# Shared PSUM banks for two partial sums, a later third block, and a gate in three pieces, in a spectral layer with a feed-forward network

## The chip, the cores and the metric

The kernel runs on one NeuronCore of one Trainium2 chip. The metric is the device time of one execution in microseconds (us), as the median of several runs. The engines are called by the profile's names: PE (matmul), PEld (the loading of PE's weights), DVE (vector), ACT (scalar), POOL (GpSimd) and SP (issues DMAs).

## What is computed

```
X = rfft(x, axis=1)                       # x is (8, 3008, 256)
Yr = Xr @ w_r - Xi @ w_i + b_r ; Yi = Xr @ w_i + Xi @ w_r + b_i
Yr, Yi = soft threshold of both at 0.01
y = irfft(Yr + 1j * Yi, n=3008, axis=1)
h = y.reshape(24064, 256) @ moe_w_in      # to 2048 features
out = (h * clip(h + 3, 0, 6) / 6) @ moe_w_out
```

All numbers are float32. The kernel keeps that precision by splitting every operand of a large product into a rounded part (`hi`) and a rest (`lo`) and by adding three matmuls (weight lo by hi, hi by lo, hi by hi, in this order) (`product`, line 137).

## The kernel before

There are two kinds of work. The *spectral* work makes `y`: for each of the 8 batches `stage1`, `middle` and `segment` do the transforms as matmuls with small tables, through the PSUM pool `ps_a`. The *units* are the feed-forward network: 47 tiles of 512 tokens by 8 pairs of 128-feature blocks, 376 units in all.

A unit's first product (256 inputs to 256 features, for 512 tokens) is a 2x2 by 2x2 product of blocks, done with seven block products in place of eight (`block(i, n, ...)`, n from 1 to 7, as in Winograd's form of Strassen's method). Each is three matmuls of 128x128 by 256 columns. `prepare` makes the seven right sides `yb` once for each tile.

- Blocks 1, 6, 7 and 4 add up in one PSUM tile, `pb`. ACT copies what stands in it after block 1 (`p1`), after 6 (`u2`), after 7 (`u3`, line 563) and after 4 (a quarter of `h`, line 594).
- Block 2 goes to the PSUM tile `pd`; DVE adds `p1` to it (a quarter of `h`, line 566).
- Block 5 goes to the PSUM tile `pc`; DVE adds `u3` (another quarter). Block 3 is then added onto `pc`; DVE adds `u2` (the last quarter).

DVE's three additions are called the p1 add, the u3 add and the u2 add below. When the four quarters of `h` are there, the *gate* follows (`gate`, a generator that is advanced at chosen places): ACT makes `r` = relu(h + 3) (line 601), DVE makes min(r, 6)·h (line 603), ACT rounds it to `gs` hi (line 130), and DVE makes the rest, `gs` lo (line 131, called the gs subtraction). A unit's second product is four *down products* (`down(i, u, dh)`), each of three matmuls of 512 columns into `po0` or `po1`; the first and the third go to `po0`, the others to `po1`. The first matmul of a down product reads `gs` hi, the second reads `gs` lo, the third `gs` hi again.

The loop at the end works on several units in one step: in step i it runs phases a and b of unit i (blocks 2, 1, then 6), phases c and d of unit i-1 (blocks 7, 5, then 4, 3), and the down products of unit i-3. `fill` puts spectral work between them. The text's order is a priority only: the framework's scheduler orders each engine's instructions by what its own model holds ready, the earlier in the text first, and fixes that order in the program. On the chip each engine then takes its queue in that order, and an instruction that waits for a semaphore holds all behind it.

PSUM has eight banks, and all are given out: `pb` two, `pd` one, `pc` one, `po0` and `po1` one each, `ps_a` two. A tile that is freed is given to the next of its name when all that read it have ended.

Of the kernel before, what the change touches and what calls it, by code (L numbers as in the profile page):

```python
# [9 lines left out]
F32 = mybir.dt.float32  # L10
# [5 lines left out]
PSUM = bass.MemoryType.PSUM  # L16
# [9 lines left out]
P = 128  # L26
# [7 lines left out]
H = T // 2  # L34
# [66 lines left out]
def spectral_ffn(ctx: ExitStack, tc: tile.TileContext, x, w_r, w_i, bias, w_in, w_out, f47, f64, g64, sgn, out):  # L101
    nc = tc.nc
# [1 line left out]
    sb = ctx.enter_context(tc.tile_pool(name="sb", bufs=1))  # L104
    dram = ctx.enter_context(tc.tile_pool(name="dram", bufs=2, space=DRAM))
    ps_b = ctx.enter_context(tc.tile_pool(name="ps_b", bufs=2, space=PSUM))
    ps_c = ctx.enter_context(tc.tile_pool(name="ps_c", bufs=1, space=PSUM))
    ps_o = ctx.enter_context(tc.tile_pool(name="ps_o", bufs=1, space=PSUM))
    ps_a = ctx.enter_context(tc.tile_pool(name="ps_a", bufs=2, space=PSUM))

# [3 lines left out]
    def space(shape, dt, name, tag=None):  # L114
        tag = tag or name
        return sb.tile(shape, dt, name=name, tag=tag, bufs=depth.get(tag, 1))
# [11 lines left out]
    def split(hi, lo, src, on=None):  # L128

        nc.scalar.copy(out=hi, in_=src)  # L130
        (on or nc.vector).tensor_tensor(out=lo, in0=src, in1=hi.bitcast(F32), op=ALU.subtract)  # L131

    def product(ps, terms, start=True, stop=True, more=False):

        todo = [p for (ah, al), (bh, bl) in terms for p in ((al, bh), (ah, bl), (ah, bh))]
        for n, (a, b) in enumerate(todo):
            nc.tensor.matmul(  # L137
                out=ps,
                lhsT=a,
                rhs=b,  # L140
                start=start and n == 0,
                stop=stop and n == len(todo) - 1,
                skip_group_check=more,
            )
# [100 lines left out]
    def turn(how=None):  # L245

        for job in list(busy):
            if next(job[0], busy) is busy:
                busy.remove(job)
                ready.add(job[1])  # L250
        if how and made[0] < 2 * nf:
            make, f = next(bands)
            g = make(f, how[made[0] % len(how)])
            next(g)
            busy.append((g, (make, f)))
            made[0] += 1
# [298 lines left out]
    hs, ps_of, keep, gs, pos = {}, {}, {}, {}, {}  # L555

    def block(i, n, ps, start):
        c, f = units[i]
        product(ps, [(tuple(t[:, f, WEIGHT[n]] for t in win_s), yb[c, n])], start=start, more=True)

    def kept(i, n, ps):
        t = keep[i, n] = space([P, H], F32, n)
        nc.scalar.copy(out=t, in_=ps)  # L563

    def added(i, u, half, ps, n):
        nc.vector.tensor_tensor(out=hs[i][:, u, half * H : (half + 1) * H], in0=ps, in1=keep.pop((i, n)), op=ALU.add)  # L566

    def phase_a(i):
        pb = ps_b.tile([P, 512], F32, name="pb")[:, :H]
        pd = ps_c.tile([P, 512], F32, name="pd")[:, :H]  # L570
        ps_of[i] = pb
        hs[i] = space([P, 2, T], F32, "h")
        block(i, 2, pd, True)
        block(i, 1, pb, True)
        kept(i, "p1", pb)
        added(i, 0, 0, pd, "p1")

    def phase_b(i):
        block(i, 6, ps_of[i], False)
        kept(i, "u2", ps_of[i])  # L580

    def phase_c(i):
        pc = ps_c.tile([P, 512], F32, name="pc")[:, :H]
        block(i, 7, ps_of[i], False)
        block(i, 5, pc, True)
        kept(i, "u3", ps_of[i])
        added(i, 1, 1, pc, "u3")
        keep[i, "pc"] = pc

    def phase_d(i):  # L590
        pb, pc = ps_of.pop(i), keep.pop((i, "pc"))
        block(i, 4, pb, False)
        block(i, 3, pc, False)
        nc.scalar.copy(out=hs[i][:, 1, :H], in_=pb)  # L594
        added(i, 0, 1, pc, "u2")

    def gate(i):

        h = hs.pop(i)
        r = space([P, 2, T], F32, "r")  # L600
        nc.scalar.activation(out=r, in_=h, func=AF.Relu, bias=three, scale=1.0)  # L601
        yield
        nc.vector.scalar_tensor_tensor(out=r, in0=r, scalar=6.0, in1=h, op0=ALU.min, op1=ALU.mult)  # L603
        t = gs[i] = space([P, 2, 2, T], F32R, "gs")
        split(t[:, 0], t[:, 1], r)
        yield

    def down(i, u, dh):
        c, f = units[i]
        ft = 2 * f + u  # L610
        first, last = f == 0 and u == 0, f == nf - 1 and u == 1
        if first:
            pos[dh] = ps_o.tile([P, 512], F32, name=f"po{dh}")
        g = gs[i]
        product(
            pos[dh],
            [(part(wout_s, slice(ft * D + dh * P, ft * D + (dh + 1) * P)), (g[:, 0, u], g[:, 1, u]))],
            start=first,
            stop=last,
        )  # L620
        if last:
            ot = space([P, T], F32, "ot")
            if dh:
                nc.vector.tensor_scalar(out=ot, in0=pos[dh], scalar1=1.0 / 6.0, scalar2=None, op0=ALU.mult)
            else:
                nc.scalar.mul(out=ot, in_=pos[dh], mul=1.0 / 6.0)
            nc.sync.dma_start(out=out[dh * P : (dh + 1) * P, c * T : (c + 1) * T], in_=ot)
# [57 lines left out]
    def fill(q):  # L685
        turn(LATE if q % 2 == 0 else None)
        for g in slots.get(q, []):
            next(g, None)

    gates = {}  # L690

    def gated(i):
        if i in gates:
            next(gates[i], None)

    n = len(units)
    for i in range(n + 3):
        for kind, f in ((in_band, i), (out_band, i - 3)):
            while 0 <= f < nf and (kind, f) not in ready:
                turn(LATE)  # L700
        if i < n:
            phase_a(i)
        gated(i - 2)
        fill(4 * i)
        if 0 <= i - 3 < n:
            down(i - 3, 0, 0)
        if 0 <= i - 1 < n:
            phase_c(i - 1)
        fill(4 * i + 1)
        if 0 <= i - 3 < n:  # L710
            down(i - 3, 0, 1)
        if i < n:
            phase_b(i)
        fill(4 * i + 2)
        if 0 <= i - 3 < n:
            down(i - 3, 1, 0)
        if 0 <= i - 1 < n:
            phase_d(i - 1)
            gates[i - 1] = gate(i - 1)
            gated(i - 1)  # L720
        fill(4 * i + 3)
        if 0 <= i - 3 < n:
            down(i - 3, 1, 1)
            gs.pop(i - 3)


def words(w):
# [42 lines left out]
```

## Time and profile before

| what | value |
|---|---|
| median of 3 runs (lowest, highest) | 2685.37 us (2683.7, 2688.47) |
| profiled execution: span from first to last instruction | 2685.1 us |
| mean granted clock of PE | 0.983 |
| busy: PE, PEld, DVE, ACT, POOL | 2575.2, 2304.1, 1975.0, 1845.8, 809.6 us |
| first matmul into `pd` (the first unit) | at 146 us |

The profiled execution has no time beside its span; the span lies 0.3 us below the median of the runs. Until about 470 us the first units run between the spectral work of the first batches and the decoding of the weights. From there to about 2300 us units and spectral work alternate, and behind 2300 us little but units is left. A row of a timeline gives the start, the duration, the engine, the line, the operation with out<-in, the shapes and how many instructions were merged; in brackets stands how long the engine was idle before it and what ended that.

### The profile page before, as it was taken

What the parts mean: (1) busy time and instruction counts of PE and PEld (TensorE: products, weight loads), DVE (VectorE), ACT (ScalarE), POOL (GpSimd) and SP (SyncE); (2) the same over time, 40 slices, a digit from 0 to 9 for tenths busy, and PEclk for the clock granted to TensorE, in tenths of its full rate; (3) what the DMA queues carried; (4) which work ended last, traced back from release to release, by engine and by line L of the source; (5) the groups of instructions that cost most, each with busy time, mean ns of one, the idle gap of its engine ahead of it and who ended that gap; (6) DMA issues with size and microseconds to landing.
All of it is one profiled execution on the core that took longest, in us unless ns stands there. A gap on an engine that the chain in (4) does not pass through costs nothing.

```text
span 2685.1 us, 44479 instructions
## 1 busy us (share of the span) xinstructions
PE 2575.2 (96%) x16432; PEld 2304.1 (86%) x16432; DVE 1975.0 (74%) x3192; ACT 1845.8 (69%) x3631; POOL 809.6 (30%) x772
## 2 busy tenths in 40 slices
PE   5778998999999999999999999999999999999999
PEld 4667887898899888898898888989888999999997
DVE  7766885777777777777777777777777777766666
ACT  5666666676777777677776777676667666677765
POOL 4254333233313432333322433243232122121210
PEclk8879999999999999999999999999999999999999
DMA  6623433232222331223222322132222121101000
GB/s 198 188 61 98 125 105 95 77 83 72 76 72 70 83 88 55 73 80 85 74 61 72 87 81 67 58 90 78 77 66 65 56 60 50 48 24 31 16 20 17
DMA packets 150178, 199.98 MB, mean 74 GB/s; under 512 B 16847, under 2 KB 104135, under 8 KB 149959
## 3 DMA queue, kind: packets, MB, share of 16 engines
q1 hardware_dynamic: 149959, 197.13, 25.6%
q8 instruction: 129, 2.11, 0.3%
q14 instruction: 90, 0.74, 0.1%
HBM read 97.45 MB, written 74.97 MB: 64 GB/s over the span
## 4 chain that ended last, share of the span: by engine, by line
PE 68%; DVE 11%; ACT 8%; issue 4%; POOL 3%; DMA 3%; SPq 0%; ACTq 0%; DVEq 0%; POOLq 0%
PE po L137 28%; PE pb L137 15%; PE ps_a L137 9%; PE pc L137 8%; PE pd L137 4%; ACT r L601 3%; DVE r L603 3%; ACT gs L130 2%; PE ps_a L502 2%; DVE gs L131 2%; PE ps_a L377 2%; DMA xin<-in_x 2%; DVE h L566 2%; DVE X L131 1%; DVE tc L427 1%
## 5 line engine op out<-in xcount | busy, mean ns | idle before, releaser
L137 PE MATMUL po<-gs,w_out_hi 128*128 128x512 f32 x3008 | 950.1, 396 | 1.0 <-DVE gs L131 1.0
L603 DVE SCALAR_TENSOR_TENSOR r<-r,h 128x1024 f32<-128x1024 f32 x376 | 476.0, 1266 | 382.8 <-ACT r L601 382.4
L137 PEld LDWEIGHTS po<-gs,w_out_hi 128*128 128x128 f32 x3008 | 568.3, 189 | 68.8 <-DVE gs L131 2.2
L137 PE MATMUL po<-gs,w_out_lo 128*128 128x512 f32 x1504 | 606.2, 403 | 1.7 <-ACT gs L130 1.7
L137 PE MATMUL pb<-yb,w_in_hi 128*128 128x256 f32 x3008 | 598.9, 280 | 1.8 <-POOL yb L131 1.8
L131 DVE TENSOR_TENSOR gs<-r,gs 128x1024 fp32r<-128x1024 f32 x376 | 477.9, 1271 | 131.6 <-ACT gs L130 128.4
L601 ACT ACTIVATE r<-h,three 128x1024 f32<-128x1024 f32 x376 | 433.2, 1152 | 201.5 <-DVE h L566 198.4
L137 PEld LDWEIGHTS pb<-yb,w_in_hi 128*128 128x128 f32 x3008 | 464.5, 189 | 51.2 <-POOL yb L131 2.1
L130 ACT CAST gs<-r 128x1024 fp32r<-128x1024 f32 x376 | 396.0, 1053 | 137.0 <-DVE r L603 129.2
L131 POOL TENSOR_TENSOR yb<-T,yb 128x256 fp32r<-128x256 f32 x188 | 208.6, 1120 | 764.0 <-ACT yb L130 763.9
L137 PE MATMUL pb<-yb,w_in_lo 128*128 128x256 f32 x1504 | 427.2, 284 | 7.4 <-ACT h L594 5.0
L566 DVE TENSOR_TENSOR h<-pc,u 128x256 f32<-128x256 f32 x752 | 313.8, 417 | 67.0 <-PE pc L137 63.5
L137 PEld LDWEIGHTS pb<-yb,w_in_lo 128*128 128x128 f32 x1504 | 284.3, 189 | 65.8 <-ACT h L594 6.6
L563 ACT COPY u<-pb 128x256 f32<-128x256 f32 x752 | 276.5, 372 | 90.5 <-PE pb L137 86.5
L137 PE MATMUL pc<-yb,w_in_hi 128*128 128x256 f32 x1504 | 298.7, 280 | 1.4 <-POOL yb L131 1.4
L137 PEld LDWEIGHTS po<-gs,w_out_lo 128*128 128x128 f32 x1504 | 284.2, 189 | 10.4 <-ACT gs L130 2.3
L137 PE MATMUL pc<-yb,w_in_lo 128*128 128x256 f32 x752 | 217.8, 290 | 15.2 <-DVE h L566 14.7
L137 PEld LDWEIGHTS pc<-yb,w_in_hi 128*128 128x128 f32 x1504 | 230.1, 190 | 2.1 <-POOL yb L131 1.6
L594 ACT COPY h<-pb 128x256 f32<-128x256 f32 x376 | 140.7, 374 | 122.4 <-PE pb L137 120.4
L137 PEld LDWEIGHTS pc<-yb,w_in_lo 128*128 128x128 f32 x752 | 141.9, 189 | 35.0 <-DVE h L566 32.4
L131 POOL TENSOR_TENSOR xs<-xin,xs 120x512 fp32r<-120x512 f32 (+1 forms) x45 | 59.1, 1313 | 352.4 <-ACT xs L130 290.6
L566 DVE TENSOR_TENSOR h<-pd,p 128x256 f32<-128x256 f32 x376 | 156.8, 417 | 7.3 <-ACT p L563 4.6
(129 smaller groups left out, 4018.0 us busy)
## 6 DMA issues: line engine op xcount, KB each, us to landing
bt<-scr SPq DMA_DIRECT2D x96, 256.0 KB, 3.0
scr<-pt SPq DMA_DIRECT2D x96, 256.0 KB, 2.0
zt<-tc SPq DMA_DIRECT2D x376, 64.0 KB, 2.0
out<-ot SPq DMA_DIRECT2D x94, 256.0 KB, 2.1
xin<-in_x SPq DMA_DIRECT2D x48, 480.0 KB, 4.5
scr<-a SPq DMA_DIRECT2D x96, 240.0 KB, 2.5
qt<-scr SPq DMA_DIRECT2D x96, 240.0 KB, 3.5
f<-in_f SPq DMA_DIRECT2D x96, 128.0 KB, 2.9
```

The source lines that it names most:

```text
L130: nc.scalar.copy(out=hi, in_=src)
L131: (on or nc.vector).tensor_tensor(out=lo, in0=src, in1=hi.bitcast(F32), op=ALU.subtract)
L137: nc.tensor.matmul(out=ps, lhsT=a, rhs=b, start=start and n == 0, stop=stop and n == len(todo) - 1, skip_group_check=more,)
L377: nc.tensor.matmul(out=psv[:, dh, :, u, :], lhsT=data[:, u, dh * P : (dh + 1) * P], rhs=f[:, u, :], start=True, stop=True,)
L427: nc.vector.tensor_tensor(out=t, in0=t, in1=c, op=ALU.subtract)
L502: nc.tensor.matmul(out=ps[:, cs * w + g * rows : cs * w + (g + 1) * rows], lhsT=qt[:rows, cs, g, dh * P : (dh + 1) * P], rhs=f47_s[2][:row ...
L563: nc.scalar.copy(out=t, in_=ps)
L566: nc.vector.tensor_tensor(out=hs[i][:, u, half * H : (half + 1) * H], in0=ps, in1=keep.pop((i, n)), op=ALU.add)
L594: nc.scalar.copy(out=hs[i][:, 1, :H], in_=pb)
L601: nc.scalar.activation(out=r, in_=h, func=AF.Relu, bias=three, scale=1.0)
L603: nc.vector.scalar_tensor_tensor(out=r, in0=r, scalar=6.0, in1=h, op0=ALU.min, op1=ALU.mult)
```

## The change

1. `pd` and `pc` of a unit become the two halves of one tile of one bank, and there are two such banks (pool `ps_c` with `bufs=2`), one for odd and one for even units.
2. Block 3 moves out of phase d into a new phase e, which stands behind the step's last down product; the u2 add and the start of the gate move with it. The copy of `pb` to `h` stays in phase d.
3. The gate has a second `yield`: its middle (DVE's min and product) is asked for behind phase c, and its third piece (the rounding to `gs` hi and the gs subtraction) behind phase b. Before, both were asked for behind phase a.

```
-    ps_c = ctx.enter_context(tc.tile_pool(name="ps_c", bufs=1, space=PSUM))
+    ps_c = ctx.enter_context(tc.tile_pool(name="ps_c", bufs=2, space=PSUM))
...
     def phase_a(i):
         pb = ps_b.tile([P, 512], F32, name="pb")[:, :H]
-        pd = ps_c.tile([P, 512], F32, name="pd")[:, :H]
+        both = ps_c.tile([P, 512], F32, name="pc")
+        pd, keep[i, "pc"] = both[:, :H], both[:, H:]
...
     def phase_d(i):
-        pb, pc = ps_of.pop(i), keep.pop((i, "pc"))
+        pb = ps_of.pop(i)
         block(i, 4, pb, False)
-        block(i, 3, pc, False)
         nc.scalar.copy(out=hs[i][:, 1, :H], in_=pb)
+
+    def phase_e(i):
+        pc = keep.pop((i, "pc"))
+        block(i, 3, pc, False)
         added(i, 0, 1, pc, "u2")
...
         nc.vector.scalar_tensor_tensor(out=r, in0=r, scalar=6.0, in1=h, op0=ALU.min, op1=ALU.mult)
+        yield
         t = gs[i] = space([P, 2, 2, T], F32R, "gs")
...
             phase_a(i)
-        gated(i - 2)
         fill(4 * i)
...
             phase_c(i - 1)
+        gated(i - 2)
...
             phase_b(i)
+        gated(i - 2)
...
             phase_d(i - 1)
-            gates[i - 1] = gate(i - 1)
-            gated(i - 1)
         fill(4 * i + 3)
         if 0 <= i - 3 < n:
             down(i - 3, 1, 1)
             gs.pop(i - 3)
+        if 0 <= i - 1 < n:
+            phase_e(i - 1)
+            gates[i - 1] = gate(i - 1)
+            gated(i - 1)
```

No instruction is added or removed on any engine; the order and the waits change. First, PE's queue from block 3 of a unit k (number 154, near the middle of the program) on, before (the first matmul of block 3 stands just ahead of the first row): block 3 in `pc_14133`, the fourth down product of unit k-2, blocks 2 and 1 of unit k+2, the first down product of unit k-1, block 7 and the start of block 5 of unit k+1.

```order
L137 MATMUL pc_14133<-yb_13743,w_in_hi_78 128x256 x2
L137 MATMUL po1_14150<-gs_14038,w_out_lo_81 128x512
L137 MATMUL po1_14150<-gs_14038,w_out_hi_80 128x512 x2
L137 MATMUL pd_14179<-yb_13512,w_in_lo_79 128x256
L137 MATMUL pd_14179<-yb_13512,w_in_hi_78 128x256 x2
L137 MATMUL pb_14178<-yb_13553,w_in_lo_79 128x256
L137 MATMUL pb_14178<-yb_13553,w_in_hi_78 128x256 x2
L137 MATMUL po0_14129<-gs_14114,w_out_lo_81 128x512
L137 MATMUL po0_14129<-gs_14114,w_out_hi_80 128x512 x2
L137 MATMUL pb_14101<-yb_13619,w_in_lo_79 128x256
L137 MATMUL pb_14101<-yb_13619,w_in_hi_78 128x256 x2
L137 MATMUL pc_14200<-yb_13677,w_in_lo_79 128x256
```

The last row, block 5 of unit k+1, is the first that needs the u2 add of unit k, and the program has a wait for DVE there. The same place now, with the waits shown; block 2 of unit k+2 is `pc_14024`:

```order
L137 MATMUL po1_13992<-gs_13922,w_out_lo_81 128x512
L137 MATMUL po1_13992<-gs_13922,w_out_hi_80 128x512 x2
L137 MATMUL pc_13873<-yb_13593,w_in_lo_79 128x256 [waits DVE_49]
L137 MATMUL pc_13873<-yb_13593,w_in_hi_78 128x256 x2
L137 MATMUL pb_14023<-yb_13402,w_in_lo_79 128x256 [waits Activation_49]
L137 MATMUL pb_14023<-yb_13402,w_in_hi_78 128x256 x2
L137 MATMUL po0_13971<-gs_14001,w_out_lo_81 128x512
L137 MATMUL po0_13971<-gs_14001,w_out_hi_80 128x512 [waits DVE_49]
L137 MATMUL pc_14024<-yb_13365,w_in_lo_79 128x256 [waits DVE_49]
L137 MATMUL pc_14024<-yb_13365,w_in_hi_78 128x256 x2
L137 MATMUL po0_13971<-gs_14001,w_out_hi_80 128x512
```

Block 3 (`pc_13873`) now stands behind the fourth down product, and the first that needs its u2 add is block 2 of unit k+2 (`pc_14024`, the same bank), with block 1 and two down matmuls between them.

Second, DVE's queue at the u2 add of the same unit k, now. It stands so before, too, except that the p1 add and the min-and-product stood the other way round:

```order
L131 TENSOR_TENSOR gs_14001<-r_13945,gs_14001 128x1024 [waits Activation_49]
L131 TENSOR_TENSOR z_14068<-zt_13788,z_14068 128x512 [waits DMAHW1_49,DMAHW2_49,DMAHW0_49,DMAHW3_49,PE_49,Activation_49]
L566 TENSOR_TENSOR h_13874<-pc_13873,u2_13920 128x256 [waits PE_49]
L566 TENSOR_TENSOR h_14025<-pc_14024,p1_14032 128x256 [waits PE_49,Activation_49]
L606 SCALAR_TENSOR_TENSOR r_14021<-r_14021,h_13874 128x1024 [waits Activation_49]
```

The gs subtraction of unit k-1 and a piece of spectral work (`z`) stand ahead of the u2 add (`u2_13920`).

Third, ACT's queue near the program's end, where there is no spectral work, before:

```order
L601 ACTIVATE r_29684<-h_29573,three_75 128x1024 [waits DVE_49,Activation_49]
L563 COPY p1_29698<-pb_29689 128x256 [waits PE_49]
L563 COPY u3_29718<-pb_29630 128x256 [waits PE_49]
L130 CAST gs_29702<-r_29684 128x1024 [waits DVE_49]
L563 COPY u2_29727<-pb_29689 128x256 [waits PE_49]
L594 COPY h_29632<-pb_29630 128x256 [waits PE_49]
```

and now:

```order
L563 COPY p1_29333<-pb_29324 128x256 [waits PE_49]
L563 COPY u3_29348<-pb_29266 128x256 [waits PE_49,Activation_49]
L604 ACTIVATE r_29322<-h_29210,three_75 128x1024 [waits DVE_49,Activation_49]
L563 COPY u2_29358<-pb_29324 128x256 [waits PE_49]
L130 CAST gs_29360<-r_29322 128x1024 [waits DVE_49]
L593 COPY h_29268<-pb_29266 128x256 [waits PE_49]
```

The copies `p1` and `u3` moved ahead of the gate's relu, and the copy `u2` of unit k+2 moved ahead of the gate's rounding (`CAST`) of unit k.

More of the change, by code (lines that the diff above doesn't have):

```diff
@@ L106, in spectral_ffn @@
     ps_b = ctx.enter_context(tc.tile_pool(name="ps_b", bufs=2, space=PSUM))
-    ps_c = ctx.enter_context(tc.tile_pool(name="ps_c", bufs=1, space=PSUM))
+    ps_c = ctx.enter_context(tc.tile_pool(name="ps_c", bufs=2, space=PSUM))
     ps_o = ctx.enter_context(tc.tile_pool(name="ps_o", bufs=1, space=PSUM))
@@ L569, in phase_a @@
         pb = ps_b.tile([P, 512], F32, name="pb")[:, :H]
-        pd = ps_c.tile([P, 512], F32, name="pd")[:, :H]
+        both = ps_c.tile([P, 512], F32, name="pc")
+        pd, keep[i, "pc"] = both[:, :H], both[:, H:]
         ps_of[i] = pb
@@ L582, in phase_c @@
     def phase_c(i):
-        pc = ps_c.tile([P, 512], F32, name="pc")[:, :H]
+        pc = keep[i, "pc"]
         block(i, 7, ps_of[i], False)
@@ L587, in phase_c, with phase_e @@
         added(i, 1, 1, pc, "u3")
-        keep[i, "pc"] = pc
     def phase_d(i):
-        pb, pc = ps_of.pop(i), keep.pop((i, "pc"))
+        pb = ps_of.pop(i)
         block(i, 4, pb, False)
+        nc.scalar.copy(out=hs[i][:, 1, :H], in_=pb)
+    def phase_e(i):
+        pc = keep.pop((i, "pc"))
         block(i, 3, pc, False)
-        nc.scalar.copy(out=hs[i][:, 1, :H], in_=pb)
         added(i, 0, 1, pc, "u2")
@@ L603, in gate @@
         nc.vector.scalar_tensor_tensor(out=r, in0=r, scalar=6.0, in1=h, op0=ALU.min, op1=ALU.mult)
+        yield
         t = gs[i] = space([P, 2, 2, T], F32R, "gs")
@@ L702, in spectral_ffn @@
             phase_a(i)
-        gated(i - 2)
         fill(4 * i)
@@ L708, in spectral_ffn @@
             phase_c(i - 1)
+        gated(i - 2)
         fill(4 * i + 1)
@@ L713, in spectral_ffn @@
             phase_b(i)
+        gated(i - 2)
         fill(4 * i + 2)
@@ L718, in spectral_ffn @@
             phase_d(i - 1)
-            gates[i - 1] = gate(i - 1)
-            gated(i - 1)
         fill(4 * i + 3)
@@ L724, in spectral_ffn @@
             gs.pop(i - 3)
+        if 0 <= i - 1 < n:
+            phase_e(i - 1)
+            gates[i - 1] = gate(i - 1)
+            gated(i - 1)
 def words(w):
```

## The prediction

> **What bounds the kernel now.** I read the shares of the page first, then the busy time by stretch, then the list of waits for PE and for its weight loading in the long middle stretch, and last single steps in the timeline.
>
> ```profile
> PE 2575.2 (96%) x16432; PEld 2304.1 (86%) x16432; DVE 1975.0 (74%) x3192; ACT 1845.8 (69%) x3631; POOL 809.6 (30%) x772
> ...
> 0.00:146.00 146.00, 92.20 (x494) 75.94 (x494) 107.48 (x174) 86.27 (x168) 60.11 (x64) 0.81 0.65 189
> 146.00:470.00 324.00, 291.17 (x1752) 254.53 (x1753) 231.65 (x363) 210.03 (x427) 126.37 (x115) 0.94 0.34 95
> 470.00:2300.00 1830.00, 1812.75 (x11780) 1632.80 (x11779) 1373.63 (x2247) 1284.67 (x2541) 551.23 (x511) 1.00 0.25 72
> 2300.00:2685.00 385.00, 379.10 (x2412) 340.82 (x2410) 262.22 (x411) 264.85 (x497) 71.86 (x82) 1.00 0.07 24
> ```
>
> The columns behind the length of a stretch are busy time of PE, PEld, DVE, ACT and POOL, then clock and DMA. From 470 us on PE is busy all but 23 us of 2215 (17.25 and 5.9). So PE's stream bounds the kernel, and an edit that only moves work can win what PE waits, and can lose whatever new waits it puts into that stream. What PE waits for between 470 and 2300 us, as the matmuls see it and as the weight loads ahead of them see it (total, times, longest):
>
> ```profile
> PE pc L137 <- DVE h L566: 12.5, 32, 1.1
> ...
> PEld pc L137 <- DVE h L566: 28.2, 56, 1.3
> PEld pb L137 <- ACT u L563: 4.4, 11, 0.9
> PEld pb L137 <- ACT p L563: 3.5, 11, 0.6
> PEld pb L137 <- ACT h L594: 2.4, 5, 0.8
> ```
>
> One wait stands out: a `pc` block that waits for an addition on DVE. It is block 3 waiting for the u3 add, as in the step at 1244 us:
>
> ```profile
> 1243.93 0.41 DVE L566 TENSOR_TENSOR h<-pc,u 128x256 f32<-128x256 f32 x1
> 1244.39 0.19 PEld L137 LDWEIGHTS pc<-yb,w_in_lo 128*128 128x128 f32 x1 [0.52 <-DVE h L566]
> 1244.40 0.39 PE L137 MATMUL pc<-yb,w_in_lo 128*128 128x256 f32 x1 [0.33 <-DVE h L566]
> ```
>
> The add ends at 1244.34 and PE goes on 0.06 us later. Now a step near the end, without spectral work:
>
> ```profile
> 2630.62 1.27 DVE L131 TENSOR_TENSOR gs<-r,gs 128x1024 fp32r<-128x1024 f32 x1 [0.45 <-ACT gs L130]
> 2630.64 0.28 PE L137 MATMUL pc<-yb,w_in_lo 128*128 128x256 f32 x1
> ...
> 2631.69 0.28 PE L137 MATMUL pd<-yb,w_in_lo 128*128 128x256 f32 x1
> 2631.80 0.41 DVE L566 TENSOR_TENSOR h<-pc,u 128x256 f32<-128x256 f32 x1
> 2632.04 0.28 PE L137 MATMUL pb<-yb,w_in_lo 128*128 128x256 f32 x1
> 2632.31 1.15 ACT L601 ACTIVATE r<-h,three 128x1024 f32<-128x1024 f32 x1 [1.09 <-DVE h L566]
> 2632.38 0.39 PE L137 MATMUL po<-gs,w_out_lo 128*128 128x512 f32 x1
> 2633.07 0.28 PE L137 MATMUL pb<-yb,w_in_lo 128*128 128x256 f32 x1
> 2633.50 1.22 DVE L603 SCALAR_TENSOR_TENSOR r<-r,h 128x1024 f32<-128x1024 f32 x1 [1.28 <-ACT r L601]
> 2634.75 1.05 ACT L130 CAST gs<-r 128x1024 fp32r<-128x1024 f32 x1 [0.75 <-DVE r L603]
> 2635.84 1.23 DVE L131 TENSOR_TENSOR gs<-r,gs 128x1024 fp32r<-128x1024 f32 x1 [0.45 <-ACT gs L130]
> 2636.91 0.28 PE L137 MATMUL pd<-yb,w_in_lo 128*128 128x256 f32 x1
> 2636.98 0.42 DVE L566 TENSOR_TENSOR h<-pc,u 128x256 f32<-128x256 f32 x1
> ```
>
> Prices from here: a block takes PE 0.35 us (2631.69 to 2632.04), a down product 0.69 (2632.38 to 2633.07), a whole step 5.22 (2631.69 to 2636.91). And there is a second ring beside PE's: u2 add, relu, min-and-product, rounding, gs subtraction, next u2 add, 5.18 us from 2631.80 to 2636.98. DVE takes the next u2 add behind the gs subtraction. Without spectral work this ring has 0.04 us to spare.
>
> **The change part by part.** No instruction comes or goes; only places in the queues and waits change.
>
> *Block 3 behind the last down product.* The u3 add gets 0.69 us more. The waits above have a mean of 0.50 (28.2 by 56) and a longest of 1.3, so most end. Bounds of the gain are the two views of the same waits, 12.5 and 28.2; I take 24, nearer the second, since PE cannot stream without weights, less some 4 for the waits over 0.69. **-24.**
>
> *The shared bank.* Before, the u2 add of unit k was next needed by block 5 of unit k+1, behind the fourth down product, blocks 2 and 1, the first down product and block 7: 0.69+0.35+0.35+0.69+0.35 = 2.43 us. Now block 2 of unit k+2 writes into that bank and waits for it, with block 1 and two down matmuls in between, 0.35+0.46 = 0.81 (so in 151 of the 270 steps between 470 and some 2345 us; in few is it over 1.5, by the order). What the add takes when DVE is free, and when it isn't:
>
> ```profile
> 1504.25 0.40 PE L137 MATMUL pc<-yb,w_in_hi 128*128 128x256 f32 x2
> ...
> 1504.68 0.43 DVE L566 TENSOR_TENSOR h<-pc,u 128x256 f32<-128x256 f32 x1 [0.71 <-PE pc L137]
> ...
> 535.49 0.40 PE L137 MATMUL pc<-yb,w_in_hi 128*128 128x256 f32 x2
> 536.85 0.42 DVE L566 TENSOR_TENSOR h<-pc,u 128x256 f32<-128x256 f32 x1
> ...
> 2342.57 0.39 PE L137 MATMUL pc<-yb,w_in_hi 128*128 128x256 f32 x2
> 2343.27 0.42 DVE L566 TENSOR_TENSOR h<-pc,u 128x256 f32<-128x256 f32 x1
> ...
> L566 DVE TENSOR_TENSOR h<-pc,u x543: 406/416/428, 473.8 to 2298.4; 128x256 f32<-128x256 f32 x181
> ...
>   PE pc L137: 49.2, 77
> ```
>
> The second of the two merged matmuls starts 0.12 behind the first, at 1504.37; the add ends at 1505.11, 0.74 later. Block 2 would start 0.12+0.81 = 0.93 behind that matmul and needs the add's end 0.06 earlier: slack 0.13. That is thin: of 543 such additions DVE idled until PE was done before 77 (last row); elsewhere it was at work until about then. In 116 of the 270 steps the u2 add ended over 0.88 us behind block 3's last matmul; the first and the last of them are the two pairs at 535 and 2342 us, 1.66 and 1.01. Together these go 57 us beyond. Bounds: 0, when 0.69 us more lets DVE's older work drain, and 57, when the queue ahead of the add (gs subtraction, spectral work) moves with it. For the ring it moves, since the u2 add starts the ring; the spectral pieces follow their own matmuls and drain in part. Halfway: **+28.** Queued behind block 2 are all later matmuls, so this is paid in full.
>
> *The gate in three pieces.* Now the copy `u2` of unit k+2 stands on ACT ahead of the rounding of unit k (in all of the last 57 steps but few before, about a quarter of them). That copy waits for block 6. From block 6 on:
>
> ```profile
> 1501.88 0.28 PE L137 MATMUL pb<-yb,w_in_lo 128*128 128x256 f32 x1
> ...
> 1502.42 0.37 ACT L563 COPY u<-pb 128x256 f32<-128x256 f32 x1 [0.38 <-PE pb L137]
> ```
>
> 0.54 to the copy, 0.37 for it, 1.09 from rounding to gs subtraction (2634.75 to 2635.84), 1.25 for this, 0.06 to PE: 3.31. PE reaches the matmul that reads it after block 6, a down product, block 4, a down product, blocks 3 and 1 and one down matmul: 0.35+0.69+0.35+0.69+0.35+0.35+0.23 = 3.01. So 0.30 is lost in a step with nothing else in it. The scheduler put blocks 7 and 5 into that gap in about 35 of the last 57 steps, which leaves about 0.1 there. Bounds 0 and 57 x 0.30 = 17; I take 0.1 for each: **+6.** In the middle stretch the first down product stands 0.35 us earlier against its unit's ring (block 2 went behind it) and the ring starts 0.69 later; spectral matmuls give most steps more than that: **+3** (0 to 8).
>
> *Copies.* `p1` comes ahead of the relu, which takes part of the 3.5 us; the `h` copy gets tighter: **-2** (-4 to +2). Before 470 us other things than these blocks bind (33 us of PE idle in 324, spread): 0, from -6 to +6.
>
> Sum: -24+28+6+3-2 = +11. 2685.1+11 = 2696 us, against a span that is 0.3 under the median of the runs.
>
> The Trainium skill, "PSUM — Partial Sum Buffer", section "PSUM bank collisions raise a hardware error", has PSUM guarded by bank and quadrant, not by address, which speaks against halves of one bank. The order agrees: block 2 of unit k+2 writes the half that the u2 add doesn't read, and waits all the same. Guarded by address, block 2 would wait for the long finished p1 add, the +28 would fall, and the sum would be -17; no run here shows that.
>
> **The rivals.**
> *DVE is in time (faster).* The u2 add is on time in over half of the steps before already (154 of 270), and the scheduler placed block 2 by what it held ready. If the shared bank costs 10 or less, the sum is -24+10+3+3-2 = -10: 2675 us. It decides when the mean loss at block 2 falls below 0.06 us a step (17 us).
> *Late in every step (much slower).* In the step above the u2 add starts 1.16 behind block 3's first matmul, just when block 2 would start (0.35+0.81); it would wait 0.42+0.06 = 0.48. If a gs subtraction or spectral piece is in the way in half of all steps by that much, 57+17 join the -24 and block 2's term is the upper bound: -24+57+17+3-2 = +51, 2736 us.
> *No change.* Waits wander from block 3 to block 2 and PE's total stays: 2685 us. The rows speak for it in so far as PE waits only 23 us in 2215.
>
> **How the numbers follow.** Forecast (slower, net +6 to +35) 0.42; DVE in time 0.30; no change 0.18; late in every step 0.10. Less than 0.2% (5.4 us) is about what a measurement of this kernel cannot tell from no change. So faster 0.30, same 0.18, slower 0.52. The range runs from 2666 (gain 28 with block 2 at 5 and the rest near 3) to 2728 (block 2 at 57, ACT's term at 10); it leaves out about 2 in 10. The forecast's own range is 2691 to 2720.
>
> **What would show it.** Right: the wait of `pc` for DVE moves to block 2, with more than 100 waits of it; block 3's waits under 5 us; in the last 57 steps a down matmul waiting for the gs subtraction, steps of 5.3. Wrong: block 2 waits less than 15 us in all, or the last steps stay at 5.22, or the first 470 us move by more than 6.

## The result, and the profile after

The changed kernel takes 2712.07 us (median of 4 runs, 2710.69 to 2715.72) beside 2686.92 us of the kernel before on the same chip (2683.7 to 2689.01): ratio 1.0097, interval 1.0083 to 1.0111, so 25 us slower. The forecast was 2696 with a range of 2666 to 2728. The profiled execution has a span of 2713.9 us, 28.8 more than the profiled one before (2685.1); that run was the longest of the four, so where I split the loss below, some 3 to 4 us of it are above the typical run. In every run whose span is on record the time is 1.8 us more than the span; the forecast of 2696, added up from a span, is 2698 as a time.

First the busy time of the changed kernel and its stretches, from the page and the view by windows (length, then PE, PEld, DVE, ACT, POOL, clock, DMA share, GB/s):

```profile
PE 2595.3 (96%) x16432; PEld 2301.2 (85%) x16432; DVE 1995.8 (74%) x3192; ACT 1846.2 (68%) x3631; POOL 813.6 (30%) x772
```

```profile
146.00:470.00 324.00, 286.33 (x1721) 248.12 (x1722) 231.07 (x357) 208.90 (x424) 126.00 (x115) 0.95 0.34 95
470.00:2300.00 1830.00, 1809.11 (x11704) 1618.83 (x11703) 1381.79 (x2234) 1273.54 (x2526) 551.97 (x511) 1.00 0.25 72
2300.00:2714.00 414.00, 408.27 (x2518) 359.77 (x2516) 276.30 (x430) 277.25 (x517) 76.27 (x83) 1.00 0.08 25
```

PE's busy time is the wrong place to look. It rose by 20 us with the same 16432 instructions, in part because a matmul whose follower comes late is shown longer, not idle (the first matmul of block 2 lasts 0.38 in the mean where the second came late, and 0.28 elsewhere). The counts say more: at 2300 us 2518 matmuls are still to do, where 2412 were left before. At the earlier 379.10 us for 2412 matmuls, 0.157 each, these 106 are 17 us: so far behind is the changed kernel at 2300 us, and the other 11 or 12 us are lost in the last stretch, among units with little spectral work.

What PE's weight loading waits for between 470 and 2300 us (total, times, longest):

```profile
PEld pc L137 <- DVE h L566: 32.4, 64, 2.1
PEld po L137 <- DVE gs L131: 8.3, 10, 1.7
PEld pb L137 <- ACT h L593: 2.2, 8, 0.5
PEld pb L137 <- ACT p L563: 1.8, 9, 0.3
```

The first row looks like the old one (28.2, 56, 1.3), but it names another block. Since `pd` and `pc` are one tile now, blocks 2, 5 and 3 are all called `pc`, and only the place in the program tells them apart. It is block 2 that waits, as here (the timeline of PE, PEld, DVE and POOL, some rows left out):

```profile
850.76 1.62 DVE L131 TENSOR_TENSOR gs<-r,gs 128x1024 fp32r<-128x1024 f32 x1
...
851.38 2.15 POOL L290 TENSOR_TENSOR xin<-xin 120x512 f32<-120x512 f32 x1
...
852.11 0.40 PE L137 MATMUL pc<-yb,w_in_hi 128*128 128x256 f32 x2
...
852.30 1.50 DVE L131 TENSOR_TENSOR X<-xi,X 128x256 fp32r<-128x256 f32 x1
...
852.93 0.40 PE L137 MATMUL po<-gs,w_out_hi 128*128 128x512 f32 x1
853.73 0.41 DVE L566 TENSOR_TENSOR h<-pc,u 128x256 f32<-128x256 f32 x1
854.19 0.19 PEld L137 LDWEIGHTS pc<-yb,w_in_lo 128*128 128x128 f32 x1 [1.30 <-DVE h L566]
854.20 0.39 PE L137 MATMUL pc<-yb,w_in_lo 128*128 128x256 f32 x1 [0.87 <-DVE h L566]
854.30 0.31 PEld L137 LDWEIGHTS pc<-yb,w_in_hi 128*128 128x128 f32 x2
854.42 0.40 PE L137 MATMUL pc<-yb,w_in_hi 128*128 128x256 f32 x2
```

At 852.11 the last two matmuls of a unit's block 3 start. DVE has a spectral subtraction in hand until 853.80, the u2 add ends at 854.14, and only 0.06 later does block 2 of the unit after next go on, in the half of the bank that this add does not read. A 512-column matmul keeps the next one off for 0.231 us where nothing waits; block 2 begins 1.27 behind the last one, so 1.04 us are lost, and its own second matmul begins 0.22 behind its first instead of 0.117: another 0.1.

The u2 add came late here because the DVE work ahead of it was slow. The spectral subtraction took 1.50 us, where the same one takes 0.42 elsewhere, and the gs subtraction 1.62, where 1.22 is usual; POOL was at work from 851.38 to 853.53. This is no single case. In the kernel before, 103 DVE instructions between 470 and 2300 us took over 0.15 us more than the same instruction takes with POOL idle, 53 us in all, and each of the 103 overlapped an instruction of POOL (404 others overlapped one and did not grow by that much). DVE's three additions, which read PSUM, never grew: the longest took 0.43. Of the 46 late starts of block 3 before, 29 (13.7 of 19.8 us) had a slowed instruction in DVE's unbroken work ahead of the add (of all 274 steps 56 had one), and of the 46 of block 2 now, 27 (10.2 of 16.1 us). No run moved POOL's work, so this is read from the traces and not tested.

To get the whole account, I took both traces' matmuls in the program's order and counted by how much each began later than 0.117 us (256 columns) or 0.231 us (512) behind the one ahead of it. For the units 45 to 318, and then for the 56 steps behind them (us):

| lost at | before | after | difference |
|---|---|---|---|
| block 3 | 25.5 | 4.1 | -21.4 |
| block 2 (shared bank) | 0 | 24.5 | +24.5 |
| down products into `po0` | 9.5 | 18.2 | +8.7 |
| block 1 (behind the `h` copy) | 2.3 | 7.2 | +4.9 |
| blocks 4 and 6 | | | -3.7 |
| other matmuls | | | +1.4 |
| units 45 to 318 in all | | | +14.4 |
| first 45 units | | | +2.9 |
| last 56 steps | | | +11.1 |

The 9.5 us at `po0` before are not a wait for `gs` lo. They are 109 starts of a second matmul, each 0.08 to 0.09 late; the gs subtraction had ended over 1.3 us earlier each time, and why they are late is not known. The changed kernel has about as many of these. New are 17 waits for `gs` lo with 8.0 us.

The last steps went from a mean of 5.43 to 5.63 us. One such step of the changed kernel, in the timeline:

```profile
2658.62 0.28 PE L137 MATMUL pc<-yb,w_in_lo 128*128 128x256 f32 x1
...
2658.87 1.23 DVE L131 TENSOR_TENSOR gs<-r,gs 128x1024 fp32r<-128x1024 f32 x1 [1.11 <-ACT gs L130]
...
2660.01 0.42 DVE L566 TENSOR_TENSOR h<-pc,u 128x256 f32<-128x256 f32 x1
2660.15 0.73 PE L137 MATMUL po<-gs,w_out_hi 128*128 128x512 f32 x2
2660.22 0.37 ACT L563 COPY u<-pb 128x256 f32<-128x256 f32 x1
2660.52 1.16 ACT L604 ACTIVATE r<-h,three 128x1024 f32<-128x1024 f32 x1
...
2661.67 0.41 DVE L566 TENSOR_TENSOR h<-pc,u 128x256 f32<-128x256 f32 x1
...
2662.00 1.22 DVE L606 SCALAR_TENSOR_TENSOR r<-r,h 128x1024 f32<-128x1024 f32 x1
...
2662.53 0.37 ACT L563 COPY u<-pb 128x256 f32<-128x256 f32 x1 [0.86 <-PE pb L137]
...
2663.25 1.05 ACT L130 CAST gs<-r 128x1024 fp32r<-128x1024 f32 x1 [0.35 <-DVE r L606]
...
2664.07 0.28 PE L137 MATMUL pc<-yb,w_in_lo 128*128 128x256 f32 x1
```

From block 3 to the next block 3 it is 5.45 us. PE waits for the ring: the gs subtraction ends at 2660.10, and the matmul that reads it starts at 2660.15. The ring in turn waits for PE: the relu ends at 2661.68, but DVE has just begun the u3 add, so the min-and-product comes 0.32 later. Before, it came 0.04 behind the relu. The u2 copy at 2662.53 stands ahead of the rounding, as forecast, and costs nothing in this step: the rounding starts 0.03 behind the min-and-product.

### The profile page after: what moved, and what is told of

The parts are those of the page before. It is cut to its first block, busy times and chain, and to the rows that moved or that the text cites. A ratio compares the mean times of both kernels' runs of the same rounds, so it can differ in the third digit from the quotient of the medians.

```text
span 2713.9 us, 44820 instructions
## 1 busy us (share of the span) xinstructions
PE 2595.3 (96%) x16432; PEld 2301.2 (85%) x16432; DVE 1995.8 (74%) x3192; ACT 1846.2 (68%) x3631; POOL 813.6 (30%) x772
## 4 chain that ended last, share of the span: by engine, by line
PE 74%; DVE 9%; ACT 5%; POOL 4%; issue 4%; DMA 3%; SPq 0%; DVEq 0%; ACTq 0%; POOLq 0%
PE po L137 31%; PE pb L137 16%; PE pc L137 13%; PE ps_a L137 9%; PE ps_a L502 3%; PE ps_a L377 2%; DMA xin<-in_x 2%; DVE gs L131 2%; DVE r L606 1%; ACT gs L130 1%; ACT r L604 1%; DVE X L131 1%; DVE z L131 1%; DVE h L566 1%; POOL yb L131 1%
## 5 line engine op out<-in xcount | busy, mean ns | idle before, releaser
L137 PE MATMUL po<-gs,w_out_hi 128*128 128x512 f32 x3008 | 976.3, 398 | 8.9 <-DVE gs L131 8.5
L137 PE MATMUL pc<-yb,w_in_hi 128*128 128x256 f32 x2256 | 441.7, 280 | 0.8 <-POOL yb L131 0.8
L137 PEld LDWEIGHTS pc<-yb,w_in_hi 128*128 128x128 f32 x2256 | 344.7, 189 | 20.6 <-POOL yb L131 1.0
L137 PE MATMUL pc<-yb,w_in_lo 128*128 128x256 f32 x1128 | 324.7, 291 | 14.4 <-DVE h L566 12.8
L566 DVE TENSOR_TENSOR h<-pc,p 128x256 f32<-128x256 f32 x376 | 158.7, 422 | 211.3 <-PE pc L137 197.2
L563 ACT COPY p<-pb 128x256 f32<-128x256 f32 x376 | 139.4, 371 | 236.8 <-PE pb L137 236.1
L137 PEld LDWEIGHTS po<-gs,w_out_lo 128*128 128x128 f32 x1504 | 284.5, 189 | 11.1 <-ACT gs L130 2.4
L137 PEld LDWEIGHTS pc<-yb,w_in_lo 128*128 128x128 f32 x1128 | 211.7, 188 | 77.3 <-DVE h L566 35.5
```

The lines of the kernel that those rows point to most:

```text
L137: nc.tensor.matmul(out=ps, lhsT=a, rhs=b, start=start and n == 0, stop=stop and n == len(todo) - 1, skip_group_check=more,)
```

## The experiments

The theories were these. *Bank*: the shared bank makes block 2 wait, and most of the loss is there. *Gate*: the third piece of the gate puts the u2 copy ahead of the rounding, and that slows the last steps. *Late block 3*: with block 3 0.69 us later, the ring beside PE starts later, and what is gained at block 3 is lost where PE next reads the ring. All runs are medians beside the kernel before on the same chip. "Middle" is units 45 to 318 and "last" the 56 steps behind, each against before, from matmul spacings as above.

| kernel | us | before | ratio (interval) | middle | last |
|---|---|---|---|---|---|
| changed kernel | 2712.07 | 2686.92 | 1.0097 (1.0083 to 1.0111) | +14.4 | +11.1 |
| separate banks | 2688.07 | 2687.24 | 1.0006 (0.9997 to 1.0015) | -4.3 | +6.1 |
| gate in two | 2713.0 | 2687.24 | 1.0101 (1.0088 to 1.0115) | +15 | +11.1 |
| shared bank alone | 2719.8 | 2687.24 | 1.0123 (1.0108 to 1.0139) | +25.3 | +6.3 |
| three-piece gate alone | 2681.9 | 2687.24 | 0.998 (0.9972 to 0.9989) | -5.0 | 0 |
| late block 3 alone | 2692.06 | 2686.66 | 1.0017 (1.0008 to 1.0026) | -0.6 | +4.5 |
| block 2 later | 2698.07 | 2685.96 | 1.0045 (1.0032 to 1.0057) | -1.6 | +11.3 |
| rounding first | 2706.35 | 2685.96 | 1.0075 (1.0061 to 1.0088) | +14.3 | +6.0 |
| separate banks, rounding first | 2686.34 | 2685.96 | 1.0002 (0.9994 to 1.0011) | -3.6 | +3.5 |
| three-piece gate, u3 add first | 2672.49 | 2685.96 | 0.9948 (0.9935 to 0.9961) | -10.7 | 0 |
| u3 add first | 2672.14 | 2686.66 | 0.9942 (0.9929 to 0.9954) | -13.3 | 0 |

**Separate banks**: the changed kernel with `pd` and `pc` in a bank each again, one of each.

```
-    ps_c = ctx.enter_context(tc.tile_pool(name="ps_c", bufs=2, space=PSUM))
+    ps_c = ctx.enter_context(tc.tile_pool(name="ps_c", bufs=1, space=PSUM))
...
-        both = ps_c.tile([P, 512], F32, name="pc")
-        pd, keep[i, "pc"] = both[:, :H], both[:, H:]
+        pd = ps_c.tile([P, 512], F32, name="pd")[:, :H]
...
-        pc = keep[i, "pc"]
+        pc = keep[i, "pc"] = ps_c.tile([P, 512], F32, name="pc")[:, :H]
```

> The changed kernel with pd and pc in one bank each again (one buffer of each, as before), late block 3 and gate in three pieces kept. Theory A, the shared bank costs what PE waits at block 2 (16.1 us at its start and 8.4 inside it between units 45 and 318): block 2 then needs no u2 add and the next to need it, block 5, stands 1.75 us behind block 3, so about 25 us go, the gain at block 3 (21 us) stays: 2665 to 2680 us, faster than both. Rival B, DVE is simply late in this order whoever waits for it: the waits go to block 5 and the time stays at 2700 to 2715 us.

It is 24 us faster than the changed kernel, so the shared bank costs about that much there. That this is also the 24.5 counted at block 2 is partly chance: in the middle separate banks save 18.7, since other waits come up, and 5.0 more in the last steps. It is not faster than the kernel before, which I had expected. The waits of its weight loading between 470 and 2300 us:

```profile
PEld pc L137 <- DVE h L566: 11.7, 16, 1.7
PEld pb L137 <- ACT p L563: 7.7, 23, 0.7
PEld po L137 <- DVE gs L131: 6.3, 11, 1.8
```

Block 3 still waits little (4.4 us), yet 11.7 us of `pc` waits are in the list, and the spacings put them at block 5: it needs the bank that the u2 add reads, and that add is late too (block 5 0.5 before, 6.7 now; `po0` 9.5 before, 15.0 now; block 6 3.4 more, block 1 2.0 more). My expectation had forgotten that the waits at `po0`, block 1 and the last steps do not come from the bank.

**Gate in two**: the changed kernel with min-and-product, rounding and gs subtraction in one piece behind phase a again.

```
         nc.vector.scalar_tensor_tensor(out=r, in0=r, scalar=6.0, in1=h, op0=ALU.min, op1=ALU.mult)
-        yield
         t = gs[i] = space([P, 2, 2, T], F32R, "gs")
...
             phase_a(i)
+        gated(i - 2)
         fill(4 * i)
...
-        gated(i - 2)
         fill(4 * i + 1)
...
-        gated(i - 2)
         fill(4 * i + 2)
```

> The changed kernel with the gate in two pieces again (min-and-product and the rest both asked for behind phase a); shared bank and late block 3 kept. As the prediction had it, the third piece of the gate puts the u2 copy ahead of the rounding on ACT: then the last 57 steps lose their 11 us and the down products in the middle some 8 us, 2690 to 2700 us. Rival: the late block 3 does that by itself, since in this kernel's order the u2 copy stands ahead of the rounding in 96% of the last 57 steps still; then 2708 to 2716 us, no difference.

No difference to the changed kernel. The u2 copy still stands ahead of the rounding in 96% of the last 57 steps. So the new order of ACT's queue comes from block 3's new place, and the gate's third piece has no part in the loss; there the prediction named the wrong part of the change.

**Shared bank alone**: the kernel before with the shared bank and nothing else.

```
-    ps_c = ctx.enter_context(tc.tile_pool(name="ps_c", bufs=1, space=PSUM))
+    ps_c = ctx.enter_context(tc.tile_pool(name="ps_c", bufs=2, space=PSUM))
...
-        pd = ps_c.tile([P, 512], F32, name="pd")[:, :H]
+        both = ps_c.tile([P, 512], F32, name="pc")
+        pd, keep[i, "pc"] = both[:, :H], both[:, H:]
...
-        pc = ps_c.tile([P, 512], F32, name="pc")[:, :H]
+        pc = keep[i, "pc"]
```

> The kernel before with the shared bank alone (block 3 in its old place, gate in two pieces). Theory A: block 2 waits for the u2 add with 0.69 us of PE work in between, so some 20 to 30 us are lost at block 2, and block 3's waits (25 us) stay: 2705 to 2720 us. Rival B (the queue on DVE is late because of the late block 3): within 5 us of before, 2682 to 2692 us.

The waits of its weight loading between 470 and 2300 us:

```profile
PEld pc L137 <- DVE h L566: 68.0, 154, 2.8
PEld pb L137 <- ACT h L594: 3.4, 11, 0.8
```

The `pc` waits went from 28.2 in 56 to 68.0 in 154. By the spacings, block 2 loses 34.7 us in units 45 to 318 and 5.6 more in the last steps, and block 3 still loses 18.1. So with block 3 in its old place the bank's price is 35 us in the middle, and only 7 of block 3's 25.5 come back for it.

**Three-piece gate alone**: the kernel before with the second `yield` and the two later places.

```
         nc.vector.scalar_tensor_tensor(out=r, in0=r, scalar=6.0, in1=h, op0=ALU.min, op1=ALU.mult)
+        yield
...
-        gated(i - 2)
         fill(4 * i)
...
+        gated(i - 2)
         fill(4 * i + 1)
...
+        gated(i - 2)
         fill(4 * i + 2)
```

> The kernel before with the gate in three pieces alone. Theory A: the rounding stays ahead of the u2 copy on ACT in 99% of steps, so nothing changes: 2682 to 2692 us. Rival: the later third piece delays the gs subtraction: down products wait, 2693 to 2705 us.

```profile
PEld pc L137 <- DVE h L566: 21.3, 48, 1.8
PEld pb L137 <- ACT p L563: 7.0, 15, 1.1
```

A gain of 0.2%, at block 3 (its starts 19.8 before, 15.5 now), where my expectation had no change, and no loss in the last steps. This pointed to DVE's order: the third piece comes later in the text, so the u3 add stands ahead of the gs subtraction on DVE in 65% of the middle steps, where it was 57% before.

**Late block 3 alone**: the kernel before with block 3, the u2 add and the gate's start behind the last down product.

```
     def phase_d(i):
-        pb, pc = ps_of.pop(i), keep.pop((i, "pc"))
+        pb = ps_of.pop(i)
         block(i, 4, pb, False)
-        block(i, 3, pc, False)
         nc.scalar.copy(out=hs[i][:, 1, :H], in_=pb)
+
+    def phase_e(i):
+        pc = keep.pop((i, "pc"))
+        block(i, 3, pc, False)
         added(i, 0, 1, pc, "u2")
...
             gs.pop(i - 3)
+        if 0 <= i - 1 < n:
+            phase_e(i - 1)
+            gates[i - 1] = gate(i - 1)
+            gated(i - 1)
```

> The kernel before with the late block 3 alone (separate banks, gate in two pieces behind phase a). Block 3's waits fall from 25 to about 4 us between units 45 and 318; in their place the ring starts 0.69 us later and blocks 5 and 6 and the down products wait some 15 us, the last 57 steps 3 to 6 us. Theory: 2684 to 2694 us, no faster than before. Rival (the late block 3 is a gain that the gate's third piece spoils): 2665 to 2678 us.

```profile
PEld pc L137 <- DVE h L566: 16.8, 22, 1.7
PEld pb L137 <- ACT p L563: 9.1, 26, 0.7
PEld po L137 <- DVE gs L131: 6.6, 9, 1.8
```

Slower by 0.17%. Block 3's 25.5 us fall to 9.5, a gain of 16; `po0` loses 5.9 more, block 5 6.7 more, block 6 4.4 more, and the last steps 4.5. So what the late block 3 gains is lost again at other places. It also changes DVE's order: the u3 add stands ahead of the gs subtraction in 86% of the middle steps, where it was 57% before (95% in the changed kernel).

**Block 2 later**: the changed kernel with block 2 and the p1 add behind phase c, so that the u2 add of the unit two before has 1.75 us.

```
-        block(i, 2, pd, True)
         block(i, 1, pb, True)
         kept(i, "p1", pb)
+        keep[i, "pd"] = pd
+
+    def phase_a2(i):
+        pd = keep.pop((i, "pd"))
+        block(i, 2, pd, True)
         added(i, 0, 0, pd, "p1")
...
             phase_c(i - 1)
+        if i < n:
+            phase_a2(i)
         gated(i - 2)
```

> The changed kernel with block 2 and the p1 add asked for behind phase c: block 2 then stands 1.75 us of PE work behind block 3, not 0.81, and the bank stays shared. Theory A (the shared bank costs because only 0.81 us are left for the u2 add): the waits at block 2 (24 us between units 45 and 318) fall under 5, the rest stays, 2686 to 2694 us. Rival (the u2 add is late by more than that, or the p1 add that is now later holds the ring): 2700 to 2715 us.

```profile
PEld po L137 <- DVE gs L131: 8.7, 9, 1.8
PEld pc L137 <- DVE h L566: 6.1, 8, 1.4
PEld pb L137 <- ACT h L597: 5.8, 15, 0.9
```

Block 2's loss falls from 24.5 to 2.4 us, with the bank still shared: what costs is not the sharing but the short cover, 0.81 us, between block 3 and the next block in the same bank. The time missed its expectation by 4 us, for the same reason as with separate banks: the losses at block 1 (10.2 in all), `po0` (8.4 more than before) and the last steps (+11.3) stay.

**Rounding first**, in the changed kernel and with separate banks: an order edge on ACT puts the u2 copy of unit k+2 behind the rounding of unit k (the lines that keep the rounding in `casts` are left out).

```
     def phase_b(i):
         block(i, 6, ps_of[i], False)
-        kept(i, "u2", ps_of[i])
+        gated(i - 2)
+        if i - 2 in casts:
+            with tc.issue_after(casts.pop(i - 2)):
+                kept(i, "u2", ps_of[i])
+        else:
+            kept(i, "u2", ps_of[i])
```

> The changed kernel with the same order edge: the rounding of unit k ahead of the u2 copy of unit k+2 on ACT in every step. Theory A: the last 57 steps lose 8 to 11 us and the down products in the middle 3 to 8 us, 2695 to 2703 us; the waits at block 2 stay. Rival (the late start of the ring alone): 2708 to 2716 us.

> The kernel with separate banks, late block 3 and gate in three pieces, in which the u2 copy of unit k+2 is queued on ACT behind the rounding of unit k in every step (an order edge, no wait). Theory A (the copy that waits for block 6 ahead of the rounding costs 6 us in the last 57 steps and some 5 in the middle): 2676 to 2684 us, the last 57 steps back at 5.22 us. Rival (the ring is late because it starts 0.69 us later, whatever the order on ACT): the last steps stay at 5.3 us, 2685 to 2692 us.

The order of ACT's queue is worth 5 us of the last steps in the changed kernel and 2.6 with separate banks, and nothing in the middle. Both missed their expectation by 2 to 3 us, and with separate banks the time lies in the rival's range, 2685 to 2692. For about 40 steps near the end of each kernel (220 us, up to 30 us ahead of PE's end) I took the mean time between one part of the ring and the next (us; an addition can start up to 0.09 ahead of the recorded end of the subtraction, which counts as negative):

| kernel | gs subtraction to next u2 add | u2 add to relu | relu to min-and-product | min-and-product to rounding | relu to next relu | last steps against before |
|---|---|---|---|---|---|---|
| before | 0.04 | 0.10 | 0.03 | 0.07 | 5.38 | |
| late block 3 alone | 0.11 | 0.16 | 0.03 | 0.03 | 5.45 | +4.5 |
| separate banks | 0.10 | 0.15 | 0.03 | 0.07 | 5.48 | +6.1 |
| separate banks, rounding first | 0.11 | 0.16 | 0.03 | 0.03 | 5.45 | +3.5 |
| changed | 0.03 | 0.19 | 0.15 | 0.10 | 5.57 | +11.1 |
| rounding first | 0.14 | 0.16 | 0.03 | 0.03 | 5.48 | +6.0 |

Each step has one relu, so the column of relus is the length of the step as ACT sees it, and it has to grow with the loss. The columns ahead of it show where the ring got longer. Where block 3 is late, ACT takes the relu behind another instruction, mostly the `p1` copy and in the changed kernel the `u3` copy: in 14 to 19 of about 40 steps it starts over 0.1 us late, before in none. And in 5 of these steps (4 in the changed kernel) DVE scales a finished output between the gs subtraction and the u2 add, before in none. In all other steps but those with a spectral instruction in that place, and one of the changed kernel with a p1 add there, DVE takes the u2 add right behind the gs subtraction, as before. In the changed kernel the min-and-product also waits behind the p1 and u3 adds. With the rounding first, this wait and the one ahead of the rounding fall (0.15 and 0.10 to 0.03), and the u2 add comes 0.11 later; these are means, and no run separates the parts.

**u3 add first**, without and with the three-piece gate: block 3 in its old place, separate banks, and an order edge on DVE that puts the gs subtraction of unit k behind the u3 add of unit k+1. Without the three-piece gate, the gate's second piece is asked for behind phase c.

```
-        added(i, 1, 1, pc, "u3")
+        third[i] = added(i, 1, 1, pc, "u3").ins
...
-        split(t[:, 0], t[:, 1], r)
+        if i + 1 in third:
+            with tc.issue_after(third.pop(i + 1)):
+                split(t[:, 0], t[:, 1], r)
+        else:
+            split(t[:, 0], t[:, 1], r)
...
             phase_a(i)
-        gated(i - 2)
         fill(4 * i)
...
             phase_c(i - 1)
+        gated(i - 2)
```

> The kernel before with the gate in three pieces and, on DVE, the gs subtraction of unit k always behind the u3 add of unit k+1 (an order edge; 65% of steps in the middle have that order anyway). Block 3 stays in its place. If the waits of block 3 (21 us with the gate in three pieces) come in part from the gs subtraction standing ahead of the u3 add, some 5 to 9 us go: 2673 to 2679 us. Rival (the add that waits for block 5 holds the gs subtraction and so the down products): 2682 to 2695 us.

> The kernel before with the order edge on DVE alone (gs subtraction of unit k behind the u3 add of unit k+1); the gate stays in two pieces, of which the second is asked for behind phase c so that the edge can be set. If the edge alone does the work: 2669 to 2677 us, like the kernel with the edge and the gate in three pieces. If the third piece of the gate is needed too (it gained 5 us by itself): 2676 to 2684 us.

The waits of the weight loading between 470 and 2300 us in the kernel with a two-piece gate:

```profile
PEld pb L137 <- ACT p L563: 8.1, 18, 1.1
PEld pb L137 <- ACT u L563: 3.7, 9, 0.7
PEld pb L137 <- ACT h L594: 2.6, 5, 0.9
PEld pc L137 <- DVE h L566: 2.5, 7, 0.6
```

The `pc` waits fall from 28.2 to 2.5 us with block 3 where it was, by DVE's order, and the last steps lose nothing; there the u3 add stood first in every step already. 2672.14 us is 0.58% less than before, the best of all kernels here; the three-piece gate adds nothing to it (2672.49). Why it works for nearly all of block 3's waits is not settled: in the kernel before, the instruction that DVE had ahead of the late u3 add was the gs subtraction 16 times (7.0 us), a spectral subtraction 16 times (7.5) and the p1 add 15 times (4.0). The edge moves only the first, and the others went with it, as the scheduler gave DVE another order: the spectral subtraction `X` stood directly ahead of the u3 add 44 times before and 9 times now. The gate's second piece behind phase c was not run without the edge; the three-piece gate, which moves it too, gained 0.2%.

## Why the prediction came out as it did

The sign held, and the two large terms came out near their sizes, though not quite for the reasons given; the sum (+11 against 28.8 in the profiled executions and 25 by the medians) was too small by the small terms.

- *Block 3, -24*: measured -21.4. Its waits are under 5 us (4.1), as said. The size is right; the reason given, 0.69 us more for the u3 add, is at most a part of it. The change also put the u3 add ahead of the gs subtraction in 95% of the middle steps, and the kernels with the u3 add first, where block 3 has no 0.69 us more, bring it from 25.5 to about 3. No run separates the two.
- *The shared bank, +28*: measured +24.5 at block 2; with separate banks the middle is 18.7 shorter. Right in place. That the size fits is partly luck, as +28 was only the middle between bounds of 0 and 57. Wrong in form: I expected over 100 waits, and the list has 64, longer ones (mean 0.51). By the spacings block 2's start was late 46 times (16.1 us) and its second matmul 86 times, by about 0.1 each (8.4 us).
- *The rule of the Trainium skill* ("PSUM — Partial Sum Buffer", section "PSUM bank collisions raise a hardware error"), by which the bank and not the address is guarded, fits the waits (24.5 us at block 2 for an add that reads the other half), but they don't test it, though the prediction let the order speak for it: the pool hands a tile on as a whole, so the program has this wait whatever the hardware guards. Whether the halves could be used at once stays open; a kernel without that wait wasn't tried.
- *First down product in the middle, +3 (0 to 8)*: measured +8.7, just above its bounds. The cover was there: before, the matmul that reads `gs` lo started 2.82 us (median) behind the gs subtraction, and in only 8 of 274 steps less than the 1.04 us (0.35 and 0.69) that I took off. What failed is that I took the ring's length as fixed. PE's way from block 3 to that matmul got 1.03 us shorter in the mean, as said, but the ring from block 3 to the end of the gs subtraction got 0.19 longer, and in the 18 steps in which PE arrives just as it ends it took 7.24 us, where the same units had 6.05 before. In 8 of these, with 6.7 of the 8.0 us lost, a slowed DVE instruction stands just ahead.
- *Last 57 steps, +6 (0 to 17)*: measured +11.1, 0.2 a step where I had taken 0.1. Steps of 5.3 were forecast; the one shown has 5.45. The mechanism was put down to the wrong part: not the gate's third piece (without it the loss is the same) but the late block 3, which changes ACT's order and by itself, with no shared bank, costs 4.5. The shared bank has a part in the last steps too, which I had not priced, having counted block 2's wait only up to 2345 us: alone it costs 6.3 there, and with separate banks the changed kernel's 11.1 become 6.1.
- *Copies, -2 (-4 to +2)*: +1.2. Blocks 4 and 6 gained 3.7, but block 1, whose bank the late `h` copy reads, lost 4.9. That the copies also stand ahead of the relu and so lengthen the ring had no price.
- *First 470 us, 0 (±6)*: +2.9 by the 45th unit.

The rivals: *DVE in time* needed a loss at block 2 of 10 or less, and it was 24.5. *Late in every step* needed the down products to lose 17 in the middle; they lost 8.7. The forecast case, +6 to +35, is what happened, near its upper end.

Under the small terms lies the ring. The prediction had measured it, 5.18 us beside a step of 5.22, and then charged the 0.69 us later start at one place only, the first down product in the middle. The runs show losses at `po0`, block 5 or block 2, block 1 and in the last steps. Late block 3 alone shows it best: 16 us gained at block 3, all but 0.6 of it lost again in the middle, and 4.5 lost in the last steps. How much of that comes from the 0.69 us and how much from the other order of ACT's and DVE's queues, which the scheduler changes with it, no run tells.

## What to carry to other kernels

When a second chain of work is nearly as long as the step of the engine that bounds the kernel, moving the consumer back to spare a wait can start that chain later, and the wait returns at another reader; look first at what stood ahead of the late producer on its own engine, and change the order there (here a gain of 0.58% with one order edge, against a loss by moving the block). Look, too, at whether that work took longer than usual and what ran beside it: here DVE's slow instructions all overlapped POOL's. Two sums that share a bank are not free because each has its half: count the work between the last reader of one and the first writer of the other, here 0.81 us, against the reader's start and length, here 0.74 when nothing is in its way. Price every place that reads a chain, not only the first, and the stretch at the end too, where little other work covers it.

## What the runs showed of the hardware that I had not expected

A group of matmuls that has waited loses more than the wait: its second matmul also begins about 0.1 us late (854.20 to 854.42 above, where 0.117 is usual). In block 2 of the changed kernel this happened 86 times, 8.4 us in units 45 to 318, a third of the block's loss; inside block 3 before it was 5.7 us. A wait that ends just in time costs it too: in 41 of the 86 the first matmul was not late (by 0.05 us or less). The rows show a pattern: behind the end of the add that releases the group, the first matmul starts no sooner than 0.054 us and the second no sooner than 0.275. In block 2 of the changed kernel 72 of 274 second matmuls start 0.276 to 0.279 us behind that end, in block 3 before 49, with the shared bank alone 98. Where the first starts 0.055 behind the add's end the second loses 0.105, at 0.074 it loses 0.086, at 0.099 it loses 0.061. A few are 0.09 late without such a wait, like the 109 at `po0` before.

So no list of waits is the loss itself. For block 3 before, the matmuls' list has 12.5 us and the weight loads' 28.2, where the spacings give 25.5; with the shared bank alone the weight loads' list has 68.0, where blocks 2 and 3 lost 52.8.
